# Feed-forward blocks: the second product from seven block products over two units, kept transposed in the expert blocks' pipeline, and turned at the end

## Chip, cores and metric

The kernel runs on one core of one Trainium2 chip. The metric is device microseconds (us) of one launch; lower is better. One profiled execution of the kernel before gives the trace that this document reads.

## What is computed

Sliding-window attention makes x (2304 tokens by 512). A mixture of 8 experts follows: probabilities by eight rounds of row and column normalisation, then for each expert two products with a ReLU between them (512 to 1024 to 512), weighted and summed. A feed-forward layer with a cosine in it ends the program, and is what is changed here:

```python
def _moe2_ref(x, w_in, w_out) -> np.ndarray:   # x 2304 x 512, d_ff = 2048
    h = x @ w_in
    g = h * np.cos(h)
    return (g @ w_out).astype(np.float32)
```

All data are float32. The kernel forms each product from a high and a low part of both operands: high by high, high by low, low by high, that is three matmuls where one would give a rounded result.

## The kernel before, in words

The 2304 tokens are three blocks of TB = 768. The phases in order are moe 0, 1, 2 and ffn 0, 1, 2. A phase walks over units of FU = 256 hidden columns: 32 units in a moe phase, 8 (numbered 32 to 39) in an ffn phase.

**First product.** In every phase a unit's hidden values come from seven block products (`product(s, m)`, m = 1 to 7) instead of eight. Each is six matmuls of 384 columns (`unit_mm`). ScalarE keeps partial sums (`keep`), VectorE adds them (`add`). The order in a unit is 5, 1, 4 (of the unit before), 2, 3, 6, 7.

**Second product in moe 1 and 2.** Two units make a pair. Its hidden values H (four quarters by two units) are weighted and then multiplied by the same kind of seven products over the pair, result transposed: `s_step` is one half (`d` = 0 or 1) of product `k`: six matmuls of 384 columns, an addition into the accumulator on VectorE, and the preparation of later products. That is: the load of the weights of k+3 (`wbX` from `wdp`, SP's queue), a subtraction in place on GpSimd for four of seven products (two instructions), the high part of k+2 (ScalarE), and the low part of k+1 (VectorE). `couple()` runs after each `product` and issues one `s_step`, so TensorE's queue alternates six matmuls of the one and six of the other, 17 couples apart. H alternates between two buffers, `cX` and `hodd`.

**Second product in moe 0 and in the ffn phases.** `batch` and `g2` take one unit: six tiles of 128 tokens, each six matmuls of 512 columns; VectorE adds the result to the accumulator, tokens on the partitions. In ffn each unit's hidden values pass through `cos_chain` in two parts of 768 columns: ScalarE's Identity, a rounding and a subtraction on VectorE, ScalarE's Sin, a multiplication on VectorE, then the high part on ScalarE and the low part on GpSimd (L955, 768 columns). The stages of a chain are set apart by `tick()`, which is called twice in a couple.

The order on each engine is the order in which the code issues it; only data and buffers make an engine wait. Background work (conversion of the ffn weights from 64 bits, `convert_f64`, and their division into high and low, `prep_ffn`) is issued in slots of moe 1 and 2.

## Time and profile before

| | us |
|---|---|
| three timed runs | 1986.12, 1986.38, 1982.77 (median 1986.12) |
| the profiled execution | 1983.78 |
| its span in the trace | 1982.0 |
| first matmul of ffn 0, from the span's start | 1584.6 |
| last matmul's end | 1977.7 |

The profiled execution is the span plus 1.8 us around it. The ffn phases are the last 397 us, a fifth of the program.

### The profile page before, as it was taken

To read this page: it belongs to the slowest core of one execution; us is meant where nothing else is said; L and a number is where in the kernel's file an instruction comes from. 1 tells how busy PE (TensorE), PEld (TensorE's weight loads), DVE (VectorE), ACT (ScalarE), POOL (GpSimd) and SP (SyncE) were. 2 spreads that over 40 slices of the span, in tenths; PEclk is the share of its full clock that TensorE was granted. 3 is DMA by queue.
4 is the path that set the end of the run, shared out by engine and by line. 5 is a ranking of instruction groups with operands and counts; after the bars stand their busy time and mean duration, and the time that the engine had idled before them with its cause. 6 is when DMAs were issued, how large, how long until landed. Compare 5 with 4: busy or idle time off the path is not lost.

```text
span 1982.0 us, 31160 instructions
## 1 busy us (share of the span) xinstructions
PE 1958.4 (99%) x10977; PEld 1823.2 (92%) x10977; DVE 1559.7 (79%) x2669; ACT 862.2 (44%) x1617; POOL 967.0 (49%) x939
## 2 busy tenths in 40 slices
PE   8999999999999999999999999999999999999999
PEld 6667899999999999999999999999999999998898
DVE  7885877777777788988988877888877776757766
ACT  6885444444444433333333433333233354554543
POOL 5673566666667545454536622545454523333221
PEclk9999999999999999999999999999999999999999
DMA  7854788888888999999999888999898765565552
GB/s 195 220 141 159 263 311 292 309 303 313 310 289 310 319 340 316 343 338 317 340 327 328 274 281 284 330 341 335 324 308 296 242 222 196 197 218 176 207 192 96
DMA packets 293755, 540.05 MB, mean 272 GB/s; under 512 B 80256, under 2 KB 141792, under 8 KB 286432
## 3 DMA queue, kind: packets, MB, share of 16 engines
q1 hardware_dynamic: 292240, 537.74, 78.6%
q8 instruction: 87, 1.43, 0.3%
q14 instruction: 68, 0.56, 0.1%
q10 hardware_dynamic: 1360, 0.33, 0.1%
HBM read 384.32 MB, written 153.67 MB: 271 GB/s over the span
## 4 chain that ended last, share of the span: by engine, by line
PE 88%; DVE 2%; DMA 1%; issue 0%; SPq 0%; POOL 0%; ACT 0%; ACTq 0%; DVEq 0%; POOLq 0%
PE gT L1105 23%; PE y_moe L966 19%; PE z_moe L966 10%; PE gT L1195 7%; PE gT L1196 7%; PE gT L1194 7%; PE y_ffn L966 5%; PE x_moe L966 5%; PE z_ffn L966 2%; PE x_ffn L966 1%; DMA wbX<-wdp 1%; SPq L96 0%; DVE waX L145 0%; DVE acc_ffn L1175 0%; DVE ta L939 0%
## 5 line engine op out<-in xcount | busy, mean ns | idle before, releaser
L1105 PE MATMUL gT<-hX,wbX 128*128 128x384 f32 x2688 | 538.3, 334 | 0.9 <-DMA wbX<-wdp 0.5
L1105 PEld LDWEIGHTS gT<-hX,wbX 128*128 128x128 f32 x2688 | 471.7, 188 | 3.5 <-DMA wbX<-wdp 1.5
L966 PE MATMUL y_moe<-xtT_moe,waX 128*128 128x384 f32 x1728 | 347.1, 335 | 0.6 <-ACT s_moe L995 0.6
L966 PEld LDWEIGHTS y_moe<-xtT_moe,waX 128*128 128x128 f32 x1728 | 304.3, 188 | 3.7 <-ACT s_moe L995 0.9
L1117 DVE TENSOR_TENSOR acc_moe<-gT,acc_moe 128x384 f32<-128x384 f32 x432 | 237.7, 550 | 77.7 <-PE gT L1105 76.0
L1196 PE MATMUL gT<-wbX,hX 128*128 128x512 f32 x660 | 258.0, 391 | 0.0
L1195 PE MATMUL gT<-wbX,hX 128*128 128x512 f32 x660 | 257.8, 391 | 0.0
L1194 PE MATMUL gT<-wbX,hX 128*128 128x512 f32 x660 | 257.7, 390 | 0.0
L995 ACT ACTIVATE s_moe<-y_moe 128x384 f32<-128x384 f32 x192 | 93.3, 486 | 345.6 <-PE y_moe L966 345.5
L1139 POOL TENSOR_TENSOR hodd<-hodd 128x384 f32<-128x384 f32 x128 | 155.4, 1233 | 139.4 <-DVE hX L1125 70.4
L1139 POOL TENSOR_TENSOR cX<-cX 128x384 f32<-128x384 f32 x128 | 146.6, 1165 | 153.6 <-DVE hX L1125 93.8
L955 POOL TENSOR_TENSOR hX<-cX,hX 128x768 fp32r<-128x768 f32 x44 | 83.5, 1914 | 249.3 <-ACT hX L952 208.6
L132 POOL TENSOR_TENSOR s<-ra 128x256 f32<-128x256 f32 x80 | 62.4, 780 | 251.3 <-DVE waX L145 178.9
L1185 DVE SCALAR_TENSOR_TENSOR acc_moe<-gT,prob,acc_moe 128x512 f32<-128x512 f32 x174 | 129.6, 747 | 37.6 <-PE gT L1196 35.8
L1196 PEld LDWEIGHTS gT<-wbX,hX 128*128 128x128 f32 x660 | 123.8, 188 | 26.0
L1194 PEld LDWEIGHTS gT<-wbX,hX 128*128 128x128 f32 x660 | 123.9, 188 | 25.4 <-DVE acc_ffn L1175 0.6
L1195 PEld LDWEIGHTS gT<-wbX,hX 128*128 128x128 f32 x660 | 123.9, 188 | 24.5
L911 ACT ACTIVATE hX<-cX 128x768 fp32r<-128x768 f32 x64 | 44.0, 687 | 218.7 <-DVE cX L998 218.7
L1125 DVE TENSOR_TENSOR hX<-cX,hX 128x768 fp32r<-128x768 f32 x112 | 132.4, 1182 | 1.1 <-ACT hX L1129 1.1
L1125 DVE TENSOR_TENSOR hX<-hodd,hX 128x768 fp32r<-128x768 f32 x112 | 127.5, 1138 | 0.9 <-ACT hX L1129 0.9
L966 PE MATMUL z_moe<-xtT_moe,waX 128*128 128x384 f32 x576 | 116.4, 335 | 0.4 <-DVE waX L145 0.2
L966 PE MATMUL z_moe<-xtB_moe,waX 128*128 128x384 f32 x576 | 115.9, 335 | 0.0
(210 smaller groups left out, 3771.9 us busy)
## 6 DMA issues: line engine op xcount, KB each, us to landing
waX<-wd SPq DMA_DIRECT2D x264, 512.0 KB, 5.5
wbX<-wdp SPq DMA_DIRECT2D x224, 512.0 KB, 6.5
wd<-waX SPq DMA_DIRECT2D x32, 1792.0 KB, 6.8
wdp<-sb SPq DMA_DIRECT2D x32, 1024.0 KB, 5.8
wdp<-wbX SPq DMA_DIRECT2D x96, 256.0 KB, 4.4
wbX<-wd SPq DMA_DIRECT2D x24, 1024.0 KB, 4.8
waX<-wd SPq DMA_DIRECT2D x88, 256.0 KB, 5.2
ra<-in_moe_w_dram SPq DMA_DIRECT2D x64, 256.0 KB, 7.4
```

What stands on the lines that cost most here:

```text
L132: nc.gpsimd.tensor_tensor(out=s4[:, o], in0=x, in1=y, op=op)
L955: eng.tensor_tensor(out=h[:, 1], in0=c, in1=h[:, 0].bitcast(F32), op=ALU.subtract)
L966: nc.tensor.matmul(ps[:, :HB], wa[:, WI[m], wl, kc, :], x[:, xl, kc, :], start=start and kc == 0 and n_ == 0, stop=stop and kc == 1 and n_ ...
L995: nc.scalar.activation(out=t["s", i], in_=ps[:, :HB], func=AF.Copy)
L1105: nc.tensor.matmul(ps[:, :HB], w[:, u, wl, d * P:(d + 1) * P], x[:, xl, u, :], start=m in (1, 5, 2) and n_ == 0, stop=m in (4, 3, 2) and n ...
L1117: nc.vector.tensor_tensor(out=a, in0=ps[:, :HB], in1=a, op=ALU.add)
L1125: nc.vector.tensor_tensor(out=x[:, 1], in0=H[:, q], in1=x[:, 0].bitcast(F32), op=ALU.subtract)
L1139: nc.gpsimd.tensor_tensor(out=H[:, t[0], c], in0=H[:, t[1], c], in1=H[:, t[2], c], op=ALU.subtract)
L1185: nc.vector.scalar_tensor_tensor(out=a, in0=ps, scalar=pe, in1=a, op0=ALU.mult, op1=ALU.add)
L1194: nc.tensor.matmul(ps, hf[f][:, 0, ts], wb[:, f, 0, :], start=f == 0, stop=False)
L1195: nc.tensor.matmul(ps, hf[f][:, 0, ts], wb[:, f, 1, :], start=False, stop=False)
L1196: nc.tensor.matmul(ps, hf[f][:, 1, ts], wb[:, f, 0, :], start=False, stop=f == 1)
```

## The change

The ffn phases' second product takes the way of moe 1 and 2: pairs of units, seven products, `s_step`, a transposed accumulator. `cos_chain` now works in place on a unit's part of H and ends at the multiplication. The low part of the operands of products 5, 7 and 4 in ffn goes to GpSimd (`ON_POOL`), of the other four to VectorE. From the last products of moe 2 on, the second product runs four couples (`LAG`) further behind. `turn` makes 128-token tiles of the finished accumulator upright again with four TensorE transposes, a copy and a store: two tiles a pair in pairs 1 to 3 of the next block, and all six of the last block at the end. `prep_ffn` prepares seven pieces of w_out for a unit, not four, with four sums on GpSimd. Loads of w_out change from one of 1 MB for each unit to seven of 512 KB for each pair. `last_row` and the final `batch` go.

```diff
-            pieces = [(x, w1d[:, o], 2) for o, x in enumerate(ops)]
-            for c in range(2):
-                x = rb[:, c].rearrange("p (k f) -> p k f", f=P)
-                pieces += [(x[:, k:k + 2], w2d[:, c, :, k * P:(k + 2) * P], 2) for k in (0, 2)]
+            pieces = [(x, w1d[:, o]) for o, x in enumerate(ops)]
+            halves = lambda x: x.rearrange("p (k f) -> p k f", f=P)
+            w2d = pair_rows(u)
+            pieces += [(halves(rb[:, f, o:o + FU]), w2d[:, SO.index(m)]) for m, f, o in ((1, 0, 0), (2, 1, 0), (4, 1, FU))]
...
-            h = new_h()
-            nc.scalar.activation(out=h[:, 0], in_=c, func=AF.Copy)
-            yield
-            eng = nc.vector if (s[:2] == ("ffn", 0) and s[2] == NU1) or s == steps[-1] else nc.gpsimd
-            eng.tensor_tensor(out=h[:, 1], in0=c, in1=h[:, 0].bitcast(F32), op=ALU.subtract)
-            chained.remove(s)
+            chained.remove(key)
...
+                    if kind == "moe":
+                        defer(2, lambda: weigh(both, both))
+                    else:
+                        tail.append(cos_chain(s, 0, H[:, 0:2, x], 1))
...
+                        nc.scalar.activation(out=H[:, 2, x], in_=ps[:, :HB], func=AF.Copy)
+                        tail.append(cos_chain(s, 1, H[:, 2:4, x], 1))
...
-        NK = 7 * NPR
+        NK = 7 * (NPR + NPF)
+        READS = {1: 0, 5: 0, 3: 1, 6: 1, 7: 1, 2: 1, 4: 1}
+        ON_POOL = (5, 7, 4)
...
+        def low_part(eng, k):
+            x, H = op_slot(k), pair_t(k // 7)
+            q = OPQ[SO[k % 7]]
+            for c in range(2) if eng is nc.gpsimd else [slice(0, 2)]:
+                eng.tensor_tensor(
+                    out=x[:, 1, c], in0=H[:, q, c], in1=x[:, 0, c].bitcast(F32), op=ALU.subtract
+                )
...
+        def turn(b, tt, ps, ks=range(KC)):
+            a = accs["ffn", b][:, :, tt * P:(tt + 1) * P]
+            for kc in ks:
+                nc.tensor.transpose(ps[:, kc * P:(kc + 1) * P], a[:, kc], ident)
...
+                if key[0] == "ffn" and key[1] and j and (i, d) in ((3, 1), (4, 0)):
+                    turn(key[1] - 1, 2 * (j - 1) + i - 3, gT[i - 1])
...
-            if couples[0] >= LEAD and sigma[0] < 2 * NK:
+            if sigma[0] <= couples[0] - LEAD - 6 - (LAG if sigma[0] >= 14 * NPR - 5 else 0):
                 s_step()
...
-        last_row()
+        while sigma[0] < 2 * NK - 4:
+            s_step()
+            tick()
+            tick()
+        b = NB - 1
...
+        for tt in range(GPB, TPB):
+            s_step()
+            turn(b, tt, ends[tt - GPB])
+        ends = [ends[3], gT[2], gT[3]]
+        for tt in range(GPB):
+            turn(b, tt, ends[tt], range(2))
+        s_step()
+        for tt in range(GPB):
+            turn(b, tt, ends[tt], range(2, KC))
```

On TensorE, in the third ffn block, the order before is a unit's first products and then its 36 matmuls of 512 columns (y, x and z are the first product's PSUM banks, gT the second's).

```order
L966 MATMUL y_ffn_32_17739<-xtT_ffn_17759,waX 128x384 x6
L966 MATMUL x_ffn_33_17882<-xtB_ffn_17636,waX 128x384 x6
L966 MATMUL z_ffn_33_17851<-xtB_ffn_17645,waX 128x384 x6
L966 MATMUL y_ffn_33_17862<-xtT_ffn_17659,waX 128x384 x6
L1194 MATMUL gT_2729<-wbX,hX 128x512
L1195 MATMUL gT_2729<-wbX,hX 128x512
L1196 MATMUL gT_2729<-wbX,hX 128x512
```

After the change the two products alternate by six matmuls there, as in moe 1 and 2, with the finished block's tiles turned between them.

```order
L1139 MATMUL gT_2725<-hX,wbX 128x384 x6
L969 MATMUL z_ffn_38_17724<-xtT_ffn_16742,waX 128x384 x6
L1139 MATMUL gT_2726<-hX,wbX 128x384 x6
L1117 MATMUL gT_2727<-ident,acc_ffn_16175 128x128 x4
L969 MATMUL y_ffn_38_17752<-xtB_ffn_16766,waX 128x384 x6
L1139 MATMUL gT_2725<-hX,wbX 128x384 x6
L1117 MATMUL gT_2728<-ident,acc_ffn_16175 128x128 x4
L969 MATMUL y_ffn_37_17606<-xtT_ffn_16942,waX 128x384 x6
```

On GpSimd, in an ffn phase before, the low parts of the chains (L955) stand in a row, with the next block's operands (L352) between them.

```order
L955 TENSOR_TENSOR hX<-cX,hX 128x768 x5
L352 TENSOR_TENSOR xtB_ffn_16610<-acc_moe_7238,xtB_ffn_16610 128x384 x2
L955 TENSOR_TENSOR hX<-cX,hX 128x768
L352 TENSOR_TENSOR xtB_ffn_16643<-acc_moe_7238,xtB_ffn_16643 128x384 x2
L955 TENSOR_TENSOR hX<-cX,hX 128x768 x8
```

After the change one pair has eight subtractions in place (L1177) and six low parts (L1107), each of 384 columns, in this order.

```order
L1177 TENSOR_TENSOR hodd<-hodd 128x384 x2
L1107 TENSOR_TENSOR hX<-hodd,hX 128x384 x2
L1177 TENSOR_TENSOR hodd<-hodd 128x384 x4
L1107 TENSOR_TENSOR hX<-hodd,hX 128x384 x2
L1177 TENSOR_TENSOR hodd<-hodd 128x384 x2
L1107 TENSOR_TENSOR hX<-hodd,hX 128x384 x2
```

At the end of the program TensorE's queue holds, after the last first product, 21 half products with nothing of the first product between them; these are the last (end names the PSUM banks that the first product has left).

```order
L1139 MATMUL gT_2725<-hX,wbX 128x384 x6
L1117 MATMUL gT_2728<-ident,acc_ffn_17315 128x128 x4
L1139 MATMUL gT_2726<-hX,wbX 128x384 x6
L1139 MATMUL gT_2727<-hX,wbX 128x384 x6
L1117 MATMUL end_19369<-ident,acc_ffn_18491 128x128 x4
L1139 MATMUL gT_2728<-hX,wbX 128x384 x6
L1117 MATMUL end_19370<-ident,acc_ffn_18491 128x128 x4
L1139 MATMUL gT_2725<-hX,wbX 128x384 x6
L1117 MATMUL end_19371<-ident,acc_ffn_18491 128x128 x4
```

Before, two units' `g2` and `last_row` stood in that place, with matmuls of 512 columns that share no bank with their neighbours.

## Rows read from the trace of the kernel before

**Rows 1.** The page: busy time by engine, and TensorE's granted clock in tenths.

```profile
PE 1958.4 (99%) x10977; PEld 1823.2 (92%) x10977; DVE 1559.7 (79%) x2669; ACT 862.2 (44%) x1617; POOL 967.0 (49%) x939
...
PEclk9999999999999999999999999999999999999999
```

**Rows 2.** Busy us and instructions in three stretches: PE, PEld, DVE, ACT, POOL; clock, DMA.

```profile
800.00:1000.00 200.00, 199.91 (x1162) 199.39 (x1161) 175.94 (x264) 70.37 (x124) 96.95 (x86) 1.00 0.93 333
1500.00:1580.00 80.00, 80.00 (x464) 80.00 (x463) 62.20 (x92) 25.11 (x40) 36.71 (x33) 1.00 0.77 263
1620.00:1940.00 320.00, 319.47 (x1605) 288.70 (x1604) 214.06 (x300) 159.09 (x241) 102.98 (x65) 1.00 0.55 193
```

**Rows 3.** TensorE's waits from 1584 to 1982 us: total, times, longest.

```profile
PE y_ffn L966 <- ACT s_ffn L995: 0.6, 1, 0.6
PE y_ffn L966 <- DVE cX L998: 0.5, 2, 0.3
```

**Rows 4.** The chain that ended last, its end: start, length in us, what.

```profile
1929.87 1.04 PE z_ffn L966 x6
...
1964.53 0.23 PE gT L1196
...
1977.45 0.24 PE gT L1209
...
1977.71 1.37 DVE acc_ffn L1175 x2
```

**Rows 5.** Timeline of TensorE: the ffn phases' first matmuls, and the last first product.

```profile
1584.61 1.29 PE L966 MATMUL z_ffn<-xtT_ffn,waX 128*128 128x384 f32 x6
...
1960.77 1.23 PE L966 MATMUL y_ffn<-xtT_ffn,waX 128*128 128x384 f32 x6
1961.83 0.39 PE L1194 MATMUL gT<-wbX,hX 128*128 128x512 f32 x1
```

**Rows 6.** Timeline of TensorE around one tile's four transposes in moe 1.

```profile
845.84 0.60 PE L884 MATMUL gT<-ident,acc_moe 128*128 128x128 f32 x4
846.20 1.29 PE L966 MATMUL z_moe<-xtB_moe,waX 128*128 128x384 f32 x6
847.33 0.85 PE L1105 MATMUL gT<-hX,wbX 128*128 128x384 f32 x4
```

**Rows 7.** The page's costliest groups: count, busy us, mean ns of one, idle before.

```profile
L1117 DVE TENSOR_TENSOR acc_moe<-gT,acc_moe 128x384 f32<-128x384 f32 x432 | 237.7, 550 | 77.7 <-PE gT L1105 76.0
...
L1125 DVE TENSOR_TENSOR hX<-cX,hX 128x768 fp32r<-128x768 f32 x112 | 132.4, 1182 | 1.1 <-ACT hX L1129 1.1
```

**Rows 8.** Lines one by one, after 1450 us: duration ns min/median/max, first and last start.

```profile
L1125 DVE TENSOR_TENSOR hX<-cX,hX x19: 941/1025/1686, 1452.2 to 1586.7; 128x768 fp32r<-128x768 f32 x19
L936 DVE TENSOR_SCALAR tb<-ta x49: 351/551/1409, 1604.7 to 1964.0; 128x768 f32<-128x768 f32 x47, 128x384 f32<-128x384 f32 x2
L939 DVE TENSOR_TENSOR ta<-ta,tb x49: 557/958/1653, 1605.3 to 1964.4; 128x768 f32<-128x768 f32 x47, 128x384 f32<-128x384 f32 x2
L945 DVE TENSOR_TENSOR cX<-cX,ta x49: 549/949/954, 1610.9 to 1968.0; 128x768 f32<-128x768 f32 x47, 128x384 f32<-128x384 f32 x2
L1139 POOL TENSOR_TENSOR cX<-cX x22: 1009/1016/1725, 1449.0 to 1579.3; 128x384 f32<-128x384 f32 x22
L352 POOL TENSOR_TENSOR xtB_ffn<-acc_moe,xtB_ffn x12: 1004/1017/1747, 1575.5 to 1832.0; 128x384 fp32r<-128x384 f32 x12
L1129 ACT ACTIVATE hX<-cX x18: 832/840/851, 1451.1 to 1582.1; 128x768 fp32r<-128x768 f32 x18
L933 ACT ACTIVATE ta<-cX,quarter x49: 617/928/948, 1601.2 to 1962.6; 128x768 f32<-128x768 f32 x47, 128x384 f32<-128x384 f32 x2
L942 ACT ACTIVATE ta<-ta x49: 510/847/850, 1609.9 to 1965.0; 128x768 f32<-128x768 f32 x47, 128x384 f32<-128x384 f32 x2
```

**Rows 9.** DMA issues: the whole run (first row), 1500 to 1584 us: median us to landing.

```profile
wbX<-wdp SPq DMA_DIRECT2D x224, 512.0 KB, 6.5
...
wbX<-wdp SPq DMA_DIRECT2D x20, 512.0 KB, 4.6
```

More of the change, by code (lines that the diff above doesn't have):

```diff
@@ L1141, in s_step @@
                         )
[L1142 to L1144 removed]
         LEAD = 14 + 3 - 6
+        LAG = 4
         couples = [0]
@@ L1160, in evac @@
             kind, b, u = s
-            if kind == "ffn":
-                first, e, p = u == NU1, None, u - NU1
-            else:
-                e, p = divmod(u, UPE)
-                first = u == 0
-            if first and tt == 0:
-                assert kind == "moe" or sigma[0] >= 2 * NK
+            e, p = divmod(u, UPE)
+            if not u and not tt:
                 accs[kind, b] = blk_tile(acc_tag[kind, b], f"acc_{kind}{b}", [P, TPB, DM])
@@ L1170, in evac @@
             i = b * TPB + tt
-            if kind == "ffn" or (b == 0 and u < UPE - 1):
-                if first:
+            if u < UPE - 1:
+                if not u:
                     nc.scalar.activation(out=a, in_=ps, func=AF.Copy)
@@ L1236, in begin_b @@
             kind, b, u = steps[n]
-            if kind == "ffn":
-                if b or u >= NU1 + 2:
-                    load_b(u)
-            elif not b:
+            if kind == "moe" and not b:
                 pre_next.append(prep_b(u))
@@ L1301, in tile_attention_moe_cos_ffn @@
                 nx = combos(nxt, xr[nxt[1]] if nxt[0] == "moe" else accs["moe", nxt[1]])
-            lag = 1 if kind == "moe" else 2
             for m in (5, 1, 4, 2, 3, 6, 0, 7):
                 if m == 0:
-                    if queue and queue[0] <= n - lag:
-                        while any(steps[queue[0]] == o for o in chained):
-                            tick()
-                        part = {0: range(GPB), 1: range(GPB, TPB)}[u] if (kind, b) == ("moe", 1) else range(TPB)
-                        if n + 1 == len(steps):
-                            part = range(GPB)
-                        batch(tiles=part)
+                    if queue and queue[0] < n:
+                        batch(tiles={0: range(GPB), 1: range(GPB, TPB)}[u] if (kind, b) == ("moe", 1) else range(TPB))
                     while later:
@@ L1342, in tile_attention_moe_cos_ffn @@
                 nx = None
-            if kind == "ffn" or not b:
+            if (kind, b) == ("moe", 0):
                 queue.append(n)
-            elif u % UPE == 0:
+            elif kind == "moe" and u % UPE == 0:
                 load_p((b - 1) * E + u // UPE + 1)
```

162 lines of the change are left out of this document (74 added, 88 removed).

## Prediction, on record before the changed kernel ran

> **What bounds the kernel now.** I read the page first, then busy time by stretch, then what TensorE waits for, and last the chain at the program's end.
>
> TensorE is busy 1958.4 of 1982.0 us, and its clock is granted in full in every slice [rows 1], so nothing here is to be had from the clock. In three stretches of moe 1, of moe 2 and of ffn it is busy 199.91 of 200, 80.00 of 80 and 319.47 of 320 us [rows 2]. In the ffn phases the profile finds three waits of it, 1.1 us together [rows 3]. So the time is the number of matmuls times what one takes, and what one takes is read from the starts, since the durations overlap. Six matmuls of 384 columns move the chain on by 1.04 us, 0.1734 us each. The 57 steps from the matmul at 1964.53 to that at 1977.45 us make 0.2267 us for 512 columns [rows 4].
>
> The check on this is the whole ffn stretch. It begins at 1584.61 [rows 5] and its last matmul ends at 1977.69 [rows 4]: 393.1 us. In it are 24 units of 42 matmuls of 384 columns (1008), 24 of 36 of 512 (864), and 17 halves of moe 2's second product, 102 of 384. That is 1110 x 0.1734 + 864 x 0.2267 = 388.4 us. Only 4.7 us of 393.1 are anything but matmuls at full rate.
>
> The other engines matter only where they would make TensorE wait. VectorE is busy 88% in the dense stretch of moe 1, 78% at the end of moe 2, and 67% in ffn; GpSimd 48%, 46% and 32% [rows 2]. TensorE lost 0.1 us in 200 at the first of these loads.
>
> **The change, part by part.**
>
> *Matmuls.* 864 of 512 columns go: 195.9 us. In their place 12 pairs of 84 matmuls of 384 columns come (1008): 174.8 us. That is 21.1 us less.
>
> *Transposes.* Eighteen tiles of four. The same four transposes stand in moe 1: from their start at 845.84, past six matmuls, to the next group's start at 847.33 it is 1.49 us [rows 6], and six matmuls alone are 1.04, so a tile costs 0.45 us, and eighteen 8.1 us.
>
> By these two the ffn stretch would be 1008 + 1008 + 102 matmuls of 384 columns, 367.3 us, and 8.1 us of transposes: 375.4 against 393.1 us, **17.7 us less**, if TensorE waits nowhere. (The 4.7 us of today are counted as gone; what comes in their place is the next three parts.)
>
> *VectorE in the ffn phases.* For a pair, without waits: six sums of the first product and fourteen into the accumulator at 0.55 us [rows 7], 11.0 us; four chains of 0.55 + 0.96 + 0.95 us, and four low parts of 0.94 us [rows 8], 9.8 and 3.8 us; the copy of one turned tile, nearest to a 0.55 us sum of fewer columns, 0.7 us. Together 25.3 us. A pair lasts 168 x 0.1734 + 2 x 0.45 = 30.0 us on TensorE. On top comes what GpSimd does to it. The low parts, with both inputs in SBUF, take 0.94 us at the least, 1.18 us in the mean and up to 1.69 us [rows 7, 8], while GpSimd is some 48% busy: 0.24 us for such an instruction. Twelve of a pair's instructions are of this sort, and four more (L936, 0.55 us, up to 1.41 [rows 8]) are stretched too: 16 x 0.24 = 3.8 us. The sum is 29.1 of 30.0 us, 97%, more than the 88% at which TensorE lost nothing in moe 1; how much later than that it begins to lose, no row shows. I take 0.25 us a pair, **3 us** for twelve, the two block changes with their five extra low parts on VectorE included. The bounds are 0 and, if each of 14 GpSimd instructions held VectorE for its whole length, far too much (below).
>
> *GpSimd in the ffn phases.* Eight subtractions and six low parts of 384 columns at 1.02 us each [rows 8]: 14.3 us a pair, 48%, spread over every second couple as the order shows. ScalarE has seven high parts (0.84), four Identity (0.93), four Sin (0.85) [rows 8] and some copies of 0.5 us, 17.5 us, 58%. Both have room; they cost nothing while the second product stays 21 couples behind. The later operands wait for a chain, whose five steps (0.93, 0.55, 0.96, 0.85, 0.95) make 4.2 us, and it is issued over four couples of 2.08 us, so it is done before it is asked for.
>
> *Background in moe 1 and 2.* Seven more GpSimd instructions (three low parts, four sums) for each of eight units lie under some 870 us in which it is half idle; behind them in its queue are subtractions that ScalarE's high parts wait for, two couples ahead of need. Three more stores a unit go into SP's queue. I take **0.5 us**; bounds 0 and 3.
>
> *Weight loads.* 84 of 512 KB for 24 of 1 MB, as in moe 2, where they land in 4.6 us [rows 9] and are asked for two products ahead, 8.3 us of TensorE. Hidden, except at the end.
>
> *The end.* After the last first product, at 1961.83 now [rows 5], 21 half products remain with nothing between them, so the other engines have 2.08 us for a product where they had 4.16. I followed the queues by hand with the durations above. For products 5, 7 and 4 of the last pair the path is two subtractions, ScalarE's high part, two low parts: 2.04 + 0.84 + 2.04 = 4.9 us, and GpSimd can do nothing else of this path meanwhile; for product 6 it is 2.04. That is 16.8 us, with eight hand-offs of some 0.1 us 17.6, against 7 x 2.08 = 14.6 us of matmuls: 3.0 us late. At the start of the end VectorE has the last chain's 2.5 us and a tile's copy ahead of a low part: 1.3 us late. Together **4.3 us**. The lower bound is 0 (GpSimd has run ahead); the upper is the loads: asked for two products ahead, with 6.5 us to landing as in the whole run [rows 9], a product would take 3.25 us, 1.2 more, for eight products 9.4 us. The load is light there, so I stay near the lower. Behind the last matmul little changes: now two sums (1.37 us [rows 4]) and a store, then two copies in a row and a store.
>
> **Sum:** -17.7 + 3 + 0.5 + 4.3 = -9.9 us on the profiled execution (1983.8), 1973.9 us. The three timed runs have a mean of 1985.1, and I put the forecast on that: **1975 us**. The median shown, 1986.1, is what faster or slower is counted from; 0.2%, 4.0 us, is about what a measurement of this kernel can tell from no change.
>
> A rule that speaks against the change: two-input instructions of VectorE and GpSimd's run 0.24 us longer by each other [rows 7, 8]. The Trainium skill, page "SBUF — State Buffer", section "SBUF: two separate sides", says that a VectorE instruction with two SBUF inputs, or in a two-port mode, and a GpSimd instruction exclude each other: whoever starts first holds the shared pair of ports to its end. The trace agrees: the longest low part, 1.69 us, is 0.94 and most of a 1.02 us subtraction. By that rule the ports would be held 13.6 + 14.3 = 27.9 of a pair's 30.0 us, which fits, barely, and the sum would stay; where it does not fit is the first rival.
>
> **The rivals.**
>
> *VectorE becomes the bound (slower).* Place: every pair of ffn. VectorE needs 25.3 us plus fourteen times what one GpSimd instruction costs it; TensorE needs 30.0. The point is 0.33 us for each GpSimd instruction; at 0.39 the gain is gone (14 x 0.06 x 12 = 10 us). The moe rows give 3.8/14 = 0.27. If VectorE waits half of each instruction, 0.51 us, a pair lasts 32.4 us and the time is 1975 - 3 + 12 x 2.4 = 2001 us. At a full 1.02 us it would be 9.6 us a pair, 115 us. Against it: twenty of VectorE's instructions read PSUM and stay at 0.55 us (0.550 in the mean), so GpSimd can run beneath them.
>
> *Small waits in each pair (no change).* The low part of product 4 (GpSimd, couple 2 of a pair) must have read H before the pair after next writes the sum of product 6 into the same place (VectorE, couple 5), and the PSUM bank of that sum is TensorE's two couples on. The four couples of LAG come out of this distance. With 0.8 us a pair lost the time is 1975 + 9.6 = 1985; some 1984.
>
> *The end waits for weights.* 9.4 for 4.3 us: 1980.
>
> *Nothing waits.* 1985.1 - 17.7 = 1967.5. For it: in moe, TensorE lost nothing at 88%.
>
> That the change does not do what it says can be read off the order: 84 matmuls of 384 columns a pair, alternating.
>
> **How the numbers follow.** Forecast 0.48, nothing waits 0.14, the end waits for weights 0.13, small waits 0.12, VectorE the bound 0.13. The range 1966 to 1986 takes in all but the last. Faster: the first three, 0.75. Same: small waits, 0.12. Slower: 0.13.
>
> **What would show it.** Right: 864 matmuls of 512 columns gone and 1008 of 384 at 0.173 us come, a first ffn matmul within a us of 1584.6, each ffn pair 30.0 to 30.5 us, VectorE above 90% busy there, a last stretch, 21 half products and eight tiles, of some 30 us rather than 25. Wrong: L1107 on VectorE or L948 with a mean above 1.3 us and TensorE waiting for `hX` or for `acc_ffn`; waits for `wbX` at the end; waits in moe 1 and 2 that were not there.

## The result and the profile after

| | us |
|---|---|
| changed kernel, four timed runs | 2011.33 to 2013.22, median 2012.30 |
| kernel before, four timed runs | 1982.77 to 1987.20, median 1986.25 |
| ratio | 1.0131, 95% interval 1.0119 to 1.0144 |
| profiled execution of the changed kernel, its span | 2012.19, 2010.4 |

The change makes the kernel 1.3% slower, 26 us; the forecast was 37 us too low. The page of the changed kernel first, by engine and with the granted clock, against [rows 1].

```profile
PE 1961.1 (98%) x11193; PEld 1848.3 (92%) x11193; DVE 1656.6 (82%) x2736; ACT 901.9 (45%) x1689; POOL 1155.8 (57%) x1119
...
PEclk8999999999999999999999999999999999999999
```

TensorE's busy time is 3 us longer and its share a point lower; VectorE and GpSimd have 97 and 189 us more. Where this lies, busy time by stretch tells (PE, PEld, DVE, ACT, POOL; clock, DMA), against [rows 2].

```profile
800.00:1000.00 200.00, 198.03 (x1150) 197.25 (x1149) 174.68 (x262) 73.08 (x132) 106.22 (x100) 1.00 0.94 340
1508.00:1588.00 80.00, 80.00 (x463) 80.00 (x462) 63.55 (x93) 25.51 (x40) 36.38 (x33) 1.00 0.80 269
1630.00:1950.00 320.00, 304.78 (x1717) 297.48 (x1716) 289.02 (x351) 178.64 (x272) 213.98 (x164) 0.99 0.72 236
```

In ffn TensorE, full before, is idle 15 of 320 us, and VectorE is at 90%, GpSimd at 67%. In moe 1 it is idle 2 of 200 us.

The bounds of the ffn stretch are TensorE's first ffn matmul (against [rows 5]) and the end of the chain that ended last (start, length, what; against [rows 4]).

```profile
1593.42 1.30 PE L969 MATMUL z_ffn<-xtT_ffn,waX 128*128 128x384 f32 x6
```

```profile
2003.30 0.57 DVE acc_ffn L1151
2003.87 0.04 issue
2003.92 0.34 PE end L1117
2004.26 0.02 issue
2004.28 0.60 ACT acc_ffn L1122
```

| stretch | before | after | difference | forecast |
|---|---|---|---|---|
| to the first ffn matmul | 1584.6 | 1593.4 | +8.8 | +0.5 |
| from there to TensorE's end | 393.1 | 410.8 | +17.8 | -10.4 |
| behind it | 4.3 | 6.1 | +1.8 | 0 |
| span | 1982.0 | 2010.4 | +28.4 | -9.9 |

What TensorE waits for from 1593 us on (total, times, longest), against 1.1 us in [rows 3]:

```profile
PE y_ffn L969 <- ACT s_ffn L998: 11.6, 12, 2.4
PE gT L1139 <- ACT hX L1164: 4.3, 3, 1.9
PE gT L1139 <- POOL hX L1107: 1.6, 4, 0.5
PE gT L1139 <- DVE acc_ffn L1151: 0.9, 2, 0.6
PE gT L1139 <- DMA wbX<-wdp: 0.7, 1, 0.7
```

The largest is for ScalarE, which is busy 56% of the time. So the next question is what ScalarE waits for, in the same stretch.

```profile
ACT ta L951 <- DVE ta L948: 86.4, 39, 3.7
ACT s_ffn L998 <- PE z_ffn L969: 27.0, 19, 2.1
ACT hX L1164 <- POOL hodd L1177: 17.8, 6, 5.0
```

L951 is the sine, L998 the copy of a partial sum that frees a bank of the first product. The sine stands at the head of ScalarE's queue until VectorE has done the chain's subtraction (L948), and the copy behind it. That the sine waits is not new: before the change it waited longer in all (here L942 and L939), while TensorE lost 1.1 us.

```profile
ACT ta L942 <- DVE ta L939: 98.2, 40, 5.7
```

So the sum of this wait by itself does not tell the loss. These are VectorE's and GpSimd's groups there (count, busy us, mean ns of one); [rows 8] have the same instructions as L939, L936, L945, L1125 and L1139. First the chain's subtraction before, from 1620 to 1940 us, then the groups after.

```profile
L939 DVE TENSOR_TENSOR ta<-ta,tb 128x768 f32<-128x768 f32 x41 | 40.7, 992 | 1.4
```

```profile
L948 DVE TENSOR_TENSOR ta<-ta,tb 128x768 f32<-128x768 f32 x48 | 69.6, 1449 | 1.6
L945 DVE TENSOR_SCALAR tb<-ta 128x768 f32<-128x768 f32 x48 | 44.2, 921 | 0.0
L1107 DVE TENSOR_TENSOR hX<-hodd,hX 128x768 fp32r<-128x768 f32 x31 | 34.3, 1105 | 0.0
L954 DVE TENSOR_TENSOR hodd<-hodd,ta 128x768 f32<-128x768 f32 x24 | 34.2, 1427 | 2.7 <-ACT ta L951 2.7
...
L1177 POOL TENSOR_TENSOR cX<-cX 128x384 f32<-128x384 f32 x48 | 66.9, 1416 | 9.8 <-DVE cX L954 9.8
L1107 POOL TENSOR_TENSOR hX<-cX,hX 128x384 fp32r<-128x384 f32 x36 | 46.6, 1313 | 63.8 <-ACT hX L1164 41.2 <-PE gT L1139 22.6
```

In the mean a subtraction of the chain takes 1.45 us for 0.99 before, the rounding 0.92 for 0.63, a multiplication 1.43 (on the other H buffer 1.21) for 0.95; GpSimd's instructions 1.2 to 1.4 for 1.02 (the median in [rows 8]). Both sides are stretched. How that reaches TensorE is read from the timeline, here in the first ffn block (start, length, engine, line; in brackets the idle time ahead and its releaser).

```profile
1658.10 0.95 DVE L945 TENSOR_SCALAR tb<-ta 128x768 f32<-128x768 f32 x1
...
1658.59 3.01 POOL L1107 TENSOR_TENSOR hX<-cX,hX 128x384 fp32r<-128x384 f32 x2
1659.08 1.65 DVE L948 TENSOR_TENSOR ta<-ta,tb 128x768 f32<-128x768 f32 x1
...
1659.31 1.20 PE L969 MATMUL y_ffn<-xtT_ffn,waX 128*128 128x384 f32 x6
...
1660.76 0.85 ACT L951 ACTIVATE ta<-ta 128x768 f32<-128x768 f32 x1 [3.04 <-DVE ta L948]
1661.51 0.47 ACT L998 ACTIVATE s_ffn<-y_ffn 128x384 f32<-128x384 f32 x1
...
1666.88 3.02 POOL L1177 TENSOR_TENSOR hodd<-hodd 128x384 f32<-128x384 f32 x2
...
1669.93 0.84 ACT L1164 ACTIVATE hX<-hodd 128x768 fp32r<-128x768 f32 x1 [4.99 <-POOL hodd L1177]
...
1670.68 0.47 ACT L998 ACTIVATE s_ffn<-z_ffn 128x384 f32<-128x384 f32 x1
1670.83 0.64 PEld L1139 LDWEIGHTS gT<-hX,wbX 128*128 128x128 f32 x4 [1.53 <-ACT hX L1164]
...
1673.15 2.00 PE L969 MATMUL x_ffn<-xtB_ffn,waX 128*128 128x384 f32 x6
```

GpSimd's low parts and VectorE's subtraction lie over each other, at 1.5 and 1.7 times their length. The sine begins 3 us after ScalarE was free, and the copy of a product that TensorE had finished at 1660.5 begins at 1661.5. Eight us on, two subtractions of GpSimd, begun when its work for the next block (L328) was done, take 3.0 us for 2.0; the high part waits 5.0 us, another copy stands behind it, and TensorE's weight loads stop for 1.5 us, its matmuls for 1.2. Soon after, at 1673.3, the granted clock falls to its lower level, 1.2 GHz, for 3.4 us: six matmuls take 2.00 us for 1.20. That happens three times in ffn (1673, 1714, 1984 us), each time after such gaps, but not after every one: the matmuls stopped for 1.75 us up to 1731.7, and no fall followed. Two groups of six move on by 3.65 us there (1673.15 to 1676.80) where they take 2.08 at the higher level; by the two levels a fall of 3.4 us costs 1.7.

### The profile page after: what moved, and what is told of

The parts are those of the page before. It is cut to its first block, busy times and chain, and to the rows that moved or that the text cites. A ratio compares the mean times of both kernels' runs of the same rounds, so it can differ in the third digit from the quotient of the medians.

```text
span 2010.4 us, 32135 instructions
## 1 busy us (share of the span) xinstructions
PE 1961.1 (98%) x11193; PEld 1848.3 (92%) x11193; DVE 1656.6 (82%) x2736; ACT 901.9 (45%) x1689; POOL 1155.8 (57%) x1119
## 4 chain that ended last, share of the span: by engine, by line
PE 74%; DVE 7%; POOL 4%; DMA 3%; issue 2%; ACT 1%; SPq 0%; ACTq 0%; POOLq 0%; DVEq 0%
PE gT L1139 26%; PE y_moe L969 18%; PE z_moe L969 9%; PE x_moe L969 4%; PE gT L1222 4%; PE gT L1221 4%; PE gT L1220 4%; DMA wbX<-wdp 3%; PE y_ffn L969 3%; DVE ta L948 1%; POOL cX L1177 1%; PE z_ffn L969 1%; POOL hX L1107 1%; POOL stT_ffn L328 1%; PE x_ffn L969 1%
## 5 line engine op out<-in xcount | busy, mean ns | idle before, releaser
L1139 PE MATMUL gT<-hX,wbX 128*128 128x384 f32 x3696 | 747.3, 336 | 11.9 <-ACT hX L1164 4.3
L1139 PEld LDWEIGHTS gT<-hX,wbX 128*128 128x128 f32 x3696 | 651.0, 189 | 21.3 <-ACT hX L1164 5.9
L1177 POOL TENSOR_TENSOR cX<-cX 128x384 f32<-128x384 f32 x176 | 212.3, 1227 | 130.5 <-DVE hX L1107 80.3
L1177 POOL TENSOR_TENSOR hodd<-hodd 128x384 f32<-128x384 f32 x176 | 220.5, 1274 | 109.5 <-DVE hX L1107 62.6
L998 ACT ACTIVATE s_moe<-y_moe 128x384 f32<-128x384 f32 x192 | 93.3, 486 | 344.4 <-PE y_moe L969 344.2
L1107 DVE TENSOR_TENSOR hX<-cX,hX 128x768 fp32r<-128x768 f32 x136 | 157.7, 1159 | 2.7 <-ACT hX L1164 2.7
L1107 DVE TENSOR_TENSOR hX<-hodd,hX 128x768 fp32r<-128x768 f32 x136 | 155.9, 1146 | 0.9 <-ACT hX L1164 0.9
L1164 ACT ACTIVATE hX<-hodd 128x768 fp32r<-128x768 f32 x154 | 128.4, 840 | 55.6 <-POOL hodd L1177 43.2
L1220 PE MATMUL gT<-wbX,hX 128*128 128x512 f32 x384 | 150.1, 391 | 0.0
L1222 PE MATMUL gT<-wbX,hX 128*128 128x512 f32 x384 | 150.1, 391 | 0.0
L1221 PE MATMUL gT<-wbX,hX 128*128 128x512 f32 x384 | 150.0, 391 | 0.0
L921 ACT ACTIVATE hX<-cX 128x768 fp32r<-128x768 f32 x64 | 44.0, 687 | 218.8 <-DVE cX L1001 218.8
L1164 ACT ACTIVATE hX<-cX 128x768 fp32r<-128x768 f32 x154 | 128.6, 839 | 25.9 <-POOL cX L1177 15.4
L969 PE MATMUL x_moe<-xtB_moe,waX 128*128 128x384 f32 x576 | 115.5, 334 | 0.0
L969 PE MATMUL y_moe<-xtB_moe,waX 128*128 128x384 f32 x576 | 115.5, 334 | 0.0
```

What stands on the lines that cost most here:

```text
L969: nc.tensor.matmul(ps[:, :HB], wa[:, WI[m], wl, kc, :], x[:, xl, kc, :], start=start and kc == 0 and n_ == 0, stop=stop and kc == 1 and n_ ...
L998: nc.scalar.activation(out=t["s", i], in_=ps[:, :HB], func=AF.Copy)
L1107: eng.tensor_tensor(out=x[:, 1, c], in0=H[:, q, c], in1=x[:, 0, c].bitcast(F32), op=ALU.subtract)
L1139: nc.tensor.matmul(ps[:, :HB], w[:, u, wl, d * P:(d + 1) * P], x[:, xl, u, :], start=m in (1, 5, 2) and n_ == 0, stop=m in (4, 3, 2) and n ...
L1164: nc.scalar.activation(out=x[:, 0], in_=H[:, OPQ[SO[(k + 2) % 7]]], func=AF.Copy)
L1177: nc.gpsimd.tensor_tensor(out=H[:, t[0], c], in0=H[:, t[1], c], in1=H[:, t[2], c], op=ALU.subtract)
```

## The experiments

Theory: VectorE's chain instructions and GpSimd's subtractions hold each other up, and ScalarE, which takes its work in order, carries each lateness on to TensorE. Rivals: the lag between operands and matmuls is too short, whatever the load; GpSimd's own queue is late; it is VectorE's total alone. Each time is that of one execution. "ffn" below is the time from TensorE's start on product 1 of the first ffn unit to its start on the last product of `unit_mm`, 374.0 us before and 373.9 after (the change's gain and its waits are of one size there). **Lost** is that length less 347.8, which it has when TensorE hardly waits (first run), for kernels made from the changed one, and less 374.0, that of the kept trace, for those made from the kernel before. It has in it what falls of the clock cost, 1.7 us each: two in the changed kernel, x3, y1, y5 and d1, three in y2 and y4, one in z1, none in the others. Busy us a pair are the sums over these phases by twelve.

| run | ffn | lost | VectorE | GpSimd | time | before, same chip |
|---|---|---|---|---|---|---|
| changed kernel | 373.9 | 26.1 | 28.1 | 19.6 | 2012.2 | |
| x1_no_cos | 347.8 | 0 | 15.3 | 16.2 | 1978.4 | 1983.3 |
| x2_no_pool_low | 354.1 | 6.3 | 25.3 | 13.0 | 1985.8 | 1983.3 |
| x3_low_on_vector | 371.1 | 23.3 | 28.0 | 13.0 | 2005.4 | 1983.3 |
| y1_sin_later | 367.3 | 19.5 | 27.8 | 20.6 | 2013.1 | 1988.0 |
| y2_round_on_scalar | 362.5 | 14.7 | 24.7 | 19.4 | 1999.4 | 1988.0 |
| y4_high_later | 379.8 | 32.0 | 27.6 | 19.4 | 2029.3 | 1988.0 |
| y5_one_of_768 | 379.0 | 31.2 | 29.4 | 16.7 | 2024.0 | 1988.0 |
| z1_vector_lighter | 357.3 | 9.5 | 25.3 | 11.6 | 1991.1 | 1987.9 |
| z2_without_sine_later | 357.2 | 9.4 | 25.4 | 13.2 | 1990.0 | 1987.9 |
| z3_with_stores | 356.1 | 8.3 | 25.3 | 11.7 | 1997.7 | 1987.9 |
| kernel before | 374.0 | 0 | 21.5 | 9.7 | 1983.8 | |
| d1_dummy_in_before | 403.0 | 29.1 | 25.1 | 26.6 | 2016.3 | 1987.9 |
| d2_memset_in_before | 379.7 | 5.7 | 23.1 | 23.3 | 1991.0 | 1988.1 |
| d3_dummy_fewer | 378.3 | 4.3 | 22.6 | 16.5 | 1989.2 | 1988.1 |

**x1_no_cos** leaves out the cosine chains, so the result lacks them.

```diff
-                        tail.append(cos_chain(s, 0, H[:, 0:2, x], 1))
+                        pass
...
-                        tail.append(cos_chain(s, 1, H[:, 2:4, x], 1))
```

> The changed kernel with the cosine chain left out (hidden values go on as they are; four fewer ScalarE and six fewer... that is two ScalarE and three VectorE instructions fewer for each half of a unit). First theory: in ffn VectorE's two-input instructions and GpSimd's hold each other up, and the delay reaches TensorE through ScalarE's queue; then with 9.8 us of VectorE's 25.3 us a pair gone each ffn phase falls from 122 to 128 us to 118 to 120, and the time to about 1983 (of the 27 us of waits in ffn some 22 go, of the 8 at the end half). Rival: the distance of the second product from the first and the reuse of the H buffers make the waits; then the phases stay at 122 or more and the time above 2000.

Busy time in ffn, columns as above:

```profile
1630.00:1950.00 320.00, 319.42 (x1856) 318.57 (x1855) 165.53 (x253) 123.06 (x205) 190.76 (x178) 1.00 0.73 245
```

TensorE is full again, with all of GpSimd's subtractions and low parts, all loads, all turned tiles and the same lag. So the second product as changed, its transposes and its loads run at full rate, and the 26 us come with the chains. Even so x1 is only 4.9 us faster than the kernel before on the same chip.

Against x1 one sees where the 26 us lie. The table has the twelve pairs from product 1 of the first ffn unit on, in us (a pair is 84 of the first product's matmuls; the last is cut at the last product's start).

| pair | 1 | 2 | 3 | 4 | 5 | 6 | 7 | 8 | 9 | 10 | 11 | 12 |
|---|---|---|---|---|---|---|---|---|---|---|---|---|
| x1_no_cos | 28.0 | 29.1 | 29.1 | 29.1 | 29.1 | 29.1 | 29.9 | 30.0 | 30.0 | 29.2 | 29.9 | 25.1 |
| changed kernel | 28.0 | 29.5 | 34.1 | 34.3 | 31.1 | 29.9 | 34.7 | 32.6 | 32.7 | 29.9 | 30.6 | 26.5 |
| VectorE busy in it | 26.3 | 23.6 | 29.7 | 32.0 | 30.5 | 25.5 | 31.5 | 30.6 | 31.9 | 25.6 | 26.0 | 24.4 |
| GpSimd busy in it | 9.6 | 14.5 | 29.1 | 21.8 | 20.4 | 17.7 | 29.4 | 21.8 | 21.0 | 17.7 | 17.2 | 15.3 |

Six pairs, 3 to 5 and 7 to 9, lose 22.3 us, and in them VectorE is busy as long as the pair lasts in x1, or longer; in 3 and 7 GpSimd is nearly as full. Pairs 3, 4 and 6 of the changed kernel by engine, columns as above:

```profile
1653.10:1687.20 34.10, 31.97 (x169) 30.52 (x168) 29.74 (x33) 15.88 (x25) 29.04 (x23) 0.95 0.65 216
1687.20:1721.50 34.30, 31.28 (x169) 30.64 (x169) 31.97 (x40) 21.04 (x31) 21.84 (x18) 0.95 0.64 215
...
1752.70:1782.50 29.80, 29.35 (x169) 29.03 (x168) 25.46 (x31) 18.61 (x30) 17.73 (x14) 1.00 0.74 247
```

In these six pairs the next block's operands are made besides: some 11 us of GpSimd's time (L328) in pairs 3 and 7 and 5 (L362) in 4 and 8, and 3.7 and 2.2 us of VectorE's (L364) in 4 and 5, 8 and 9. Pairs 10 to 12, with the same chains and low parts and no next block, lose 0.7 to 1.4 us each. So the load fits in the mean of twelve pairs and not in half of them. No run leaves the next block's operands out or moves them.

**x2_no_pool_low** leaves out the low parts that GpSimd makes, a term of three of the seven products.

```diff
-                if on_pool(k + 2):
-                    low_part(nc.gpsimd, k + 2)
```

> The changed kernel without GpSimd's low parts in ffn (products 5, 7 and 4 take an old low part; 6 of GpSimd's 14 instructions a pair are left out, VectorE's work is the same). If the two engines hold each other up: the VectorE instructions with two inputs in SBUF shrink from some 1.4 us towards 1.15 us, the ffn phases to 119 to 121 us, the time to about 1990. If VectorE by itself is overloaded (its own 25.3 us a pair in an unlucky order): no change there, 2005 or more.

20 of the 26 us go, 3.4 of them the two falls of the clock, which x2 does not have. No instruction of VectorE's is removed, and yet it is busy 2.8 us a pair less: the chain's subtraction takes 1.20 us for 1.45, the rounding 0.60 for 0.92, its own low parts 1.00 to 1.01 for 1.11 to 1.17.

**x3_low_on_vector** gives those low parts to VectorE instead.

```diff
-        ON_POOL = (5, 7, 4)
+        ON_POOL = ()
```

> The changed kernel with all seven low parts on VectorE (as in moe 1 and 2), a complete computation. VectorE gets 2.8 us a pair more of its own (28.1 of 30.0), GpSimd 6.1 us less (8.2). If the two holding each other up is the cause: fewer waits, about 2000. If VectorE's own load is: VectorE is then over its limit in each pair, 2020 to 2045.

Three instructions a pair more, and VectorE's busy time does not move: what the low parts cost it directly is what they had cost it by hold-up from GpSimd. The loss falls by 2.8 us only, and the time, 2005.4, lies between the two expectations. So GpSimd is not a place where this work is free.

**y1_sin_later** issues the sine two ticks later in its chain.

```diff
             nc.vector.tensor_tensor(out=ta, in0=ta, in1=tb, op=ALU.subtract)
             yield
             yield
+            yield
+            yield
```

> The changed kernel with ScalarE's Sin (and the multiplication behind it) issued one couple later, a complete computation. The profile puts 11.6 us of TensorE's waits in ffn on the first product's copies (L998), which stand behind a Sin that waits for VectorE. If ScalarE's queue is what carries the delay to TensorE: these waits fall below 4 us and the time to some 2002. If VectorE and GpSimd together simply need more than the 30 us of a pair: the waits move to another place, the ffn phases stay within 2 us, 2009 to 2014.

TensorE's waits, from 1593 us on:

```profile
PE gT L1141 <- ACT hX L1166: 5.6, 3, 2.8
PE z_ffn L971 <- DVE hodd L1003: 3.1, 2, 1.5
PE gT L1141 <- DVE acc_ffn L1153: 2.5, 5, 0.7
...
PE y_ffn L971 <- ACT s_ffn L1000: 0.6, 1, 0.6
```

The wait for the copies goes from 11.6 to 0.6 us: ScalarE's order was its cause. But ffn gets back 6.6 us only, since TensorE now waits for high parts, sums and low parts instead. The total did not fall, and missed the 2002 us expected: moe 1 and 2, which the edit does not touch, took 7.7 us more than in the changed kernel (moe 1 471.7 for 466.2).

**y2_round_on_scalar** adds the rounding constant on ScalarE (Identity with a bias), so that one VectorE instruction does what two did.

```diff
+            nc.scalar.activation(out=tb, in_=ta, func=AF.Identity, bias=magic)
...
-            nc.vector.tensor_scalar(
-                out=tb, in0=ta, scalar1=MAGIC, scalar2=MAGIC, op0=ALU.add, op1=ALU.subtract
-            )
-            nc.vector.tensor_tensor(out=ta, in0=ta, in1=tb, op=ALU.subtract)
+            nc.vector.scalar_tensor_tensor(
+                out=ta, in0=tb, scalar=MAGIC, in1=ta, op0=ALU.subtract, op1=ALU.subtract
+            )
```

> The changed kernel with the cosine's rounding on ScalarE (a second Identity that adds the rounding constant, 0.93 us) and one VectorE instruction where there were two (0.55 and 0.96 us become one of 0.96): a complete computation, VectorE 2.2 us a pair less by itself and four instructions a pair fewer that GpSimd can hold up, ScalarE 3.7 us more (21 of 30). If VectorE with what GpSimd costs it is over its limit: the ffn phases fall to 118 to 121 us, about 1998. If ScalarE's queue is the matter: no gain or a loss, 2010 to 2018.

VectorE is 3.4 us a pair lighter, 11.4 us of ffn are back, and TensorE waits 3.5 us for ScalarE's copies where it waited 11.6, although ScalarE has four instructions a pair more. Of what is left 8.2 us lie in pairs 3 and 7, a fall of the clock in each. VectorE has room there, GpSimd hardly any; pair 3:

```profile
1653.00:1686.30 33.30, 31.61 (x171) 30.71 (x170) 25.55 (x30) 20.15 (x29) 28.60 (x22) 0.95 0.67 222
```

TensorE waits there for high parts that wait for GpSimd's subtractions, and for GpSimd's low parts. So in these two pairs GpSimd's own queue is late.

**y4_high_later** prepares a product's high part, and GpSimd's low part behind it, half a product later, in moe 1 and 2 as well: `k + 1` at `d == 0`, where the changed kernel has `k + 2` at `d == 1`.

```diff
+            if d == 0 and 0 <= k + 1 < NK:
+                settle(k + 1)
+                x, H = op_slot(k + 1), pair_t((k + 1) // 7)
+                nc.scalar.activation(out=x[:, 0], in_=H[:, OPQ[SO[(k + 1) % 7]]], func=AF.Copy)
+                if on_pool(k + 1):
+                    low_part(nc.gpsimd, k + 1)
...
```

> The changed kernel with ScalarE's high part (and GpSimd's low part) issued half a product later, behind one more first product, a complete computation. If a high part that waits for GpSimd's subtraction holds up ScalarE's queue: TensorE's waits for hX on ScalarE and for L998 go down, about 2006. If not: 2010 to 2015, with more waits for hX.

Slower than either expectation: by 6 us in ffn, where TensorE waits 7.1 us for GpSimd's low parts for 1.6, and by 12.7 us in moe 1 and 2. Less distance costs time. Whether more than the changed kernel has would win some of the 26 us back was not run; x1 shows that this distance is enough without the chains.

**y5_one_of_768** lets GpSimd do its subtractions and low parts as one instruction of 768 columns, not two of 384.

```diff
-            for c in range(2) if eng is nc.gpsimd else [slice(0, 2)]:
+            for c in [slice(0, 2)]:
...
-                    for c in range(2):
+                    for c in [slice(0, 2)] if k + 3 >= 7 * NPR else range(2):
```

> The changed kernel with each pair of GpSimd instructions of 384 columns in ffn as one of 768 (1.84 us in the kernel before's L955, against 2 x 1.02), a complete computation. Seven GpSimd instructions a pair, not fourteen: if the number of times that the engines pass each other counts, some 2005; if the time for which GpSimd holds VectorE counts, the longest VectorE instruction grows from 1.8 to 2.7 us and the time stays at 2008 to 2016.

GpSimd is busy 2.9 us a pair less, and VectorE 1.3 us more: the chain's subtraction goes to 1.53 and the rounding to 1.14 us. ffn is 5 us worse, and the time, 2024.0, is above both ranges. The chain's longest subtraction is 2.5 us, near the 2.7 of the second theory: a GpSimd instruction twice as long holds VectorE up longer, and in the sum that weighs more than the shorter queue of GpSimd.

**z1_vector_lighter** joins y2, y1 and x3; **z2_without_sine_later** joins y2 and x3. **z3_with_stores** adds to z1 that `prep_ffn` stores a piece one piece later and that a turned tile goes to a row buffer, from which it is stored in rows of 2 KB and not four pieces of 512 B.

```diff
-                if n_:
+                if n_ > 1:
                     store()
...
-                nc.sync.dma_start(out=out[i * P:(i + 1) * P, :].rearrange("p (k j) -> p k j", k=KC), in_=a)
+                nc.sync.dma_start(out=out[i * P:(i + 1) * P, :], in_=o)
```

> Three edits to the changed kernel: all low parts on VectorE, the rounding's sum moved to ScalarE so that one VectorE instruction does the rest of rounding and subtraction, and the sine two ticks later. VectorE by its own durations: 25.3 - 4 x 0.55 + 3 x 0.94 = 25.9 us a pair; GpSimd 8.2 us, 27%. Theory (VectorE's total with the hold-ups, and ScalarE's queue waiting on it): the three ffn phases fall from 374 to 353 to 358 us, the time to 1990 to 1995 us. Rival (TensorE waits because the operands' chain of engines is too long, whatever VectorE's load): above 365 us.

> As z1_vector_lighter, the sine in its old place. If the sine at the head of ScalarE's queue holds up the copies of the first product only because VectorE is late, then with VectorE relieved the waits for s_ffn, 11.6 us in the changed kernel, are under 4 us and the three ffn phases are within 3 us of z1_vector_lighter; if the place of the sine is a cost of its own, they are 5 us or more longer.

> As z1_vector_lighter, and two edits outside the ffn pairs: prep_ffn's stores go into SP's queue one piece later, and a turned tile is copied to a row buffer of its own, so that its store reads 2 KB of one partition in one piece and not four of 512 B. Expected: moe 1 from 466 to 469 us in the runs so far back to 463 to 464, the end behind the last matmul from 6.0 to 5 us, together 3 to 5 us less than z1_vector_lighter. If the weights in moe 1 are late by the number of transfers and not by a store that waits at the head of SP's queue, moe 1 stays at 466 or more.

z1 and z2 get 16.6 us of ffn back, and are within 0.1 us of each other. That is in part chance: z1 has a fall of the clock, 1.7 us, and z2 none. The sine's place still tells in what TensorE waits for: 6.0 us for the copies in z2, against an expectation of under 4, and 0.6 in z1, which waits for VectorE's results instead (7.0 us). z2 comes to 2.1 us over the kernel before on the same chip, inside what a measurement can tell; no version that computes everything beat the kernel before. z3 missed both of its aims: moe 1 and 2 took 8 us more than in z1, not 3 to 5 less, and the end behind the last matmul was 6.4 us, not 5. Neither miss rules out the cause it was aimed at. y1 has 7.7 us more in moe 1 and 2 than the changed kernel with no edit there, so one execution tells little of the stores in SP's queue. And z3's row buffer holds two tiles, so that the last copies wait until an earlier tile has been stored from it:

```profile
1992.12 0.60 ACT L1133 ACTIVATE rows<-gT 128x512 f32<-128x512 f32 x1 [2.14 <-DMA out_dram<-rows]
```

The stores themselves are shorter in z3: 2.1 us from issue to landing in the median for 2.9 in z1, and 3.1 us for 4.2 from the last one's issue to the end of the span. Without the copy's wait z3's end would be some 4.3 us (an estimate, 6.4 less 2.1).

**p1_prep_in_before** gives the kernel before `prep_ffn`'s three more stores and four more GpSimd sums a unit, their results unused.

```diff
+                if o:
+                    pieces.append((t[:, w], extra[:, o - 1], 2))
...
+                if 7 <= n_ < 11:
+                    sums(n_ - 7)
```

> The kernel before with the changed kernel's preparation in moe 1 and 2 (three more pieces of a unit, four more GpSimd sums, three more stores, at its pace; the three pieces are stored and not used). If the preparation is what made moe 1 4.8 us longer (466.3 for 461.5 us): moe 1 at 465 to 467 us and the time about 1990. If that was chance: 1985 to 1987.

By its own marks p1 speaks for chance: moe 1 is 463.6 us, not 465 to 467, and the time 1986.9. Moe 1 is 2.1 us and moe 2 1.0 longer than in the trace of the kernel before, but d1, d2 and d3 below, whose code in moe is that of the kernel before, have 1.5 to 2.6 us more than that trace as well. What p1 does show is smaller. TensorE waits 1.4 us for VectorE's sums (`acc_moe`) in moe 1 and 2, as in the changed kernel (1.2), where the kernel before and d1 to d3 have 0.2. Its waits for the weights (`wbX`) differ among all of these: 0.5 us before, 2.0 to 2.4 in d1 to d3, 1.0 in p1, 2.5 in the changed kernel, 1.5 to 8.3 in those made from it. One of them stands out in the changed kernel, from TensorE's timeline:

```profile
857.90 1.31 PE L1139 MATMUL gT<-hX,wbX 128*128 128x384 f32 x6 [1.97 <-DMA wbX<-wdp]
```

and the chain that leads to it begins with the load itself, 12 us from issue to landing, where the median is 5.9:

```profile
845.86 11.99 DMA wbX<-wdp
```

**d1, d2 and d3** take the kernel before, without any of the change, and add GpSimd work in ffn that nothing uses: 14 subtractions of 384 columns a pair, 14 fills of 1024 columns that read nothing, 6 subtractions.

```diff
+                if kind == "ffn" and (b or u > NU1):
+                    d = dm[0]
+                    nc.gpsimd.tensor_tensor(out=d[:, :HB], in0=d[:, HB:2 * HB], in1=d[:, 2 * HB - P:3 * HB - P], op=ALU.subtract)
```

In d2 the last line is `nc.gpsimd.memset(d, 0.0)`; d3 has the condition `m in (5, 2, 6)` beside the others.

> The kernel before, with one GpSimd subtraction of 128x384 (two SBUF inputs, result used by nothing) added behind each first product of the ffn phases from the second unit on: 14 for two units, as many as the change brings. Nothing of the change is in it. Theory (GpSimd's two-input instructions stretch VectorE's by themselves): the chain's subtraction, 0.99 us in the mean before, goes to 1.3 us or more, the multiplication, 0.95 us, likewise, the rounding from 0.63 to 0.8 or more; VectorE's busy time there rises from 67% to about 80%, which still fits, so the time stays within 4 us of before. Rival (the stretch comes of the order of the changed kernel, chains and low parts issued together): means within 0.1 us of before. A time more than 10 us over before would say that the length of the chains, not VectorE's total, makes TensorE wait.

> As d1_dummy_in_before, but each added GpSimd instruction only writes: a fill of 128x1024, 0.96 us as the single one in d1_dummy_in_before's trace, so GpSimd's queue is as full as there. If VectorE is held up by GpSimd's reading and writing of its operands, the chain's subtraction is back near 0.99 us (1.60 in d1_dummy_in_before), the sum of VectorE's waits is gone, and the time falls by the 12 us that TensorE waited for VectorE there, to about 2000 us; what is left is GpSimd's own queue (low parts behind the added work). If any GpSimd instruction holds VectorE up, the subtraction stays at 1.5 us or more and the time at 2012 to 2018. If GpSimd's queue was all of it, the subtraction falls and the time stays at 2012 or more.

> As d1_dummy_in_before with 6 added subtractions for two units in place of 14: GpSimd at some 51% there, as the prediction had it for the change (48%). If the loss goes with the number of GpSimd instructions, 28.4 x 6/14 = 12 us over the kernel before; if TensorE loses only from a point on, because VectorE with 75% has room, within 4 us of before, with the subtraction between 1.1 and 1.4 us.

The chain's instructions on VectorE, first in d1, then in d2, then in d3, then TensorE's longest waits in d1:

```profile
L939 DVE TENSOR_TENSOR ta<-ta,tb 128x768 f32<-128x768 f32 x42 | 67.3, 1602 | 1.4
...
L936 DVE TENSOR_SCALAR tb<-ta 128x768 f32<-128x768 f32 x42 | 33.8, 806 | 5.9 <-ACT ta L933 5.6
```

```profile
L939 DVE TENSOR_TENSOR ta<-ta,tb 128x768 f32<-128x768 f32 x45 | 47.3, 1051 | 1.6
L936 DVE TENSOR_SCALAR tb<-ta 128x768 f32<-128x768 f32 x45 | 43.8, 974 | 5.5 <-ACT ta L933 5.2
```

```profile
L939 DVE TENSOR_TENSOR ta<-ta,tb 128x768 f32<-128x768 f32 x45 | 52.1, 1159 | 1.6
```

```profile
PE y_ffn L966 <- DVE cX L998: 10.9, 18, 0.9
PE gT L1196 <- POOL hX L955: 8.1, 4, 2.1
```

d1 costs as much as the whole change, 28 us, although VectorE is busy only 25.1 us of TensorE's 31.2 a pair; its expectation, that this fits, fell, and so did "VectorE's total alone". The path is another than in the changed kernel: TensorE waits for VectorE's sums and for GpSimd's low parts, and 0.6 us for ScalarE's copies. d2 loses 5.7 us: TensorE no longer waits for GpSimd, and the subtraction is back at 1.05 us. So it is GpSimd's reading that stretches VectorE's subtraction. How much of the 29 us that is, d2 does not settle, because reading also makes GpSimd's queue fuller: a subtraction takes 1.23 us, a fill 1.01, and GpSimd is busy 26.6 us a pair for 23.3. Of d1's loss 18.6 us lie in four pairs (3, 5, 7, 9) in which GpSimd is busy 30.3 to 31.4 us, as long as such a pair lasts before (31.2 to 31.6); pair 3:

```profile
1656.60:1693.00 36.40, 33.48 (x157) 29.12 (x157) 24.63 (x31) 13.44 (x20) 31.37 (x25) 0.95 0.46 160
```

d2's fullest pairs have 28.1. So the rival "GpSimd's own queue is late" stands for these pairs, as in y2. By d3 the loss is not in proportion: 6 instructions cost 4.3 us, 14 cost 29.1. (In whole time, against the kernel before on the same chip, d2 is 2.9 and d3 1.0 us longer, within the 4.4 us by which executions of the kernel before differ; but TensorE's waits in ffn are 4.9 and 4.3 us, for 1.1 before.) The Trainium skill, page "SBUF — State Buffer", section "SBUF: two separate sides", says that a VectorE instruction with two SBUF inputs is shut out only by a GpSimd instruction that reads SBUF, one in a two-port mode by any. The traces agree: the fills leave the two-input subtraction nearly alone (0.99 us before, 1.05) and stretch the one-input rounding (0.63 before, 0.97), if that is in such a mode, which no trace names.

## Why the prediction was wrong, point by point

*Matmuls* and *Transposes* were right. (Two of the prediction's sums are off by 0.1 us: 388.3 for 388.4, 1967.4 for 1967.5. Nothing hangs on it.) By their sums the stretch here called ffn would be 346.8 us (375.4 less the first couple, 2.1 us, the last first product, 1.1, and the end, 25.4); x1 has 347.8.

*VectorE in the ffn phases* is the step that failed: "I take 0.25 us a pair, **3 us** for twelve". It measured 26.1 us for twelve, 2.2 a pair, of which 3.4 us are two falls of the clock after waits of this kind. The load was nearly right in the mean, 28.1 us busy a pair for 29.1, and the mean was the error. The sum "Together 25.3 us" has no term for the next block's operands. They come on top in six of the twelve pairs, and there VectorE is busy 29.7 to 32.0 us where TensorE needs 29.1 to 30.0; these pairs lose 22.3 of the 26.1 us. With 3.7 and 2.2 us for them the sum of 29.1 would have been 32.8 and 31.3 in pairs 4 and 5, over the 30.0; VectorE measured 32.0 and 30.5. The other pairs, where the load does fit, lose 0 to 1.4 us each. On the way to TensorE ScalarE takes part: each chain crosses between it and VectorE four times, and the copies stand behind the sine (y1). Why such a pair loses up to 5.2 us, more than VectorE's excess, is not shown.

The sentence of the first rival that named "0.33 us for each GpSimd instruction" as the point below which all fits failed with it, since it too goes by the mean: the changed kernel's 28.1 us a pair are 0.20 us for each of the fourteen over 25.3, and d1's and x2's means fit equally well (25.1 and 25.3 us) with 29.1 us lost in the one and 6.3 in the other. The rival itself, *VectorE becomes the bound*, is what happened, but in half of the pairs and not, as it had it, in every pair; in 3 and 7 GpSimd is nearly as full. Its price for the pairs, 12 x 2.4 = 28.8 us, is near the 26.1 measured by luck, since it is spread over all twelve; what puts 2012 above its 2001 lies outside them.

*GpSimd in the ffn phases* was to be 14.3 us a pair and "cost nothing". It was 19.6 us in the mean: its instructions are stretched as VectorE's are, and the next block's operands, some 16 us a block, come on top, so that pairs 3 and 7 have 29.1 and 29.4 us. x2 prices its six low parts at 20 us with their hold-up.

"It is done before it is asked for" held for most operands (TensorE waits 6 us for operands against 11.6 for copies), but "both have room", said of ScalarE too, missed that the copies which free the first product's banks share its queue with the chain.

*Small waits in each pair*: its places show next to nothing (0.6 us for the sum of product 6, `y_ffn` after `hodd`).

*Background in moe 1 and 2*, 0.5 us, bounds 0 and 3, measured 5.2. Of this p1 shows some 1.2 us, waits for VectorE's sums; 2.0 us more than before are waits for the weights, which differ from execution to execution by as much. The rest is open; in all kernels made from the changed one moe 1 is 464.8 us or more, for 461.5 to 463.4 with the code of the kernel before.

*The end*, 4.3 us, measured 8.2: from 1970.7 to 2004.3 us is 33.6 for 25.4 at full rate, 1.7 of it the clock's fall at 1984 after a wait of 1.85 us for a high part. The path through GpSimd was the one that I followed, but its pairs of instructions take 2.7 us under VectorE's, where I put 2.04. The hand-offs, put at 0.1 us without a row, are 0.02 to 0.04 us in the chain at the end. *The end waits for weights* did not come: 0.7 us.

"Behind the last matmul little changes" missed 1.8 us. The last sum must be turned before it can be copied: sum, transposes, two copies in a row, three stores. The last store, in pieces of 512 B, takes 4.2 us from its issue to the end of the span, where a store of 2 KB rows took 2.9 before.

That leaves 3.5 us ahead of all this: moe 0's first product begins at 159.6 us for 156.1. In the profiled execution the clock stood at its lower level for 13.7 us from 14.4 us on, for 3.4 us in the kernel before. Kernels with the same code in that place had none (x2), 6.8 (x3) and 3.4 us (z1), and began that product at 155.8 to 156.2 us; so it belongs to the execution, not to the change.
